# Decoding weights in pairs, and moving additions, splits and products from GpSimd to VectorE, in a kernel of decay attention and two feed-forwards

## The chip, the cores and the metric

The kernel runs on one core of a Trainium2 chip. The metric is the device time of one execution in microseconds (us); for the kernel before, three runs gave 1018.64 to 1020.18 us, median 1019.32.

## The reference

Three parts follow one another, all in float32 (inputs r, k, v are 4 x 8 x 768 x 48; the tokens are 3072, the model width 384):

```
state = w * state + k_t v_t^T                       # for every batch and head, 768 steps
y_t   = r_t (state + (u * k_t) v_t^T)
x  = (h * clip(h + 3, 0, 6) / 6) @ w_out,  h = y @ w_in       # 384 -> 2048 -> 384
out = (sigmoid(x @ w_gate) * (x @ w_val)) @ w_out2            # 384 -> 1536 -> 384
```

The weights come as float64. The kernel gets them as pairs of 32-bit words and makes float32 of them itself.

## The kernel before, in words

**Products.** A float32 matrix product is made of three float32r products (high x high, high x low, low x high), so every operand is split into a high part (a rounded copy) and a low part (the rest, a subtraction). A weight tile `w` holds both parts of 128 x 384 weights.

**Decoding.** `fetch` loads one tile of 128 x 384 doubles (`raw`, 384 KB). `decode` moves tiles through three slots. First slot: ScalarE reads the high words (`a`, L74) and the low words (`e`, L75). Second slot: VectorE clamps (L81), shifts (L83), puts the sign in (L85), each an instruction for each tile in the slot, and GpSimd adds the rounding (L87). Third slot: ScalarE copies the high part into `w` (L126), VectorE subtracts for the low part (L137). There are 68 tiles: 32 for the first feed-forward (kinds "i" and "o", two per step f), 36 for the second ("g", "v", "p").

**Attention.** The 24 chunks of 128 tokens go in the order (place in the sequence, batch). For each chunk `prep` has parts: 0 scales r and k by powers of the decay (VectorE, L272) and multiplies r by k and by u (GpSimd, L273, L274); 1 sums over a head (VectorE, L280); 2 puts the sums on reversed diagonals `ae` and `ao` (ScalarE L291, GpSimd L287 for `ao` of chunks 0 to 7); 3 scales the keys (GpSimd, L293). Stage A is 8 products and two masked copies on VectorE (L304, L305). Stage U adds to the state `Zc` on VectorE (L327, L328), and ScalarE then copies the two halves into a block-diagonal matrix `Zd` (L330). Stage Y multiplies `Zd` with r (four products of 112 x 112), then adds `ae` and `ao` times v, and sends the result through `ysb` (L349) and four small DMAs (L354) into the feed-forward's input `xf`.

**Order.** The schedule is by hand (`manual_schedule`): every engine runs its instructions in the order in which the code emits them, and so does the queue of DMA issues on SyncE. Ahead of the first feed-forward step ("the head") stand the loads, chunks 0 to 3 and six calls of `slots(1)`. Then come 6 blocks of 512 tokens with 16 steps each, and 6 blocks of the second feed-forward with 12 steps each. A step i of the first feed-forward emits: the product `h` (9 matmuls), ReLU on ScalarE (L521), `t` on VectorE (L522), the split of `t` into `gh` (ScalarE, L386) and `gl` (GpSimd, L387), a stage of attention (one per step in steps 2 to 13, in the order A, U, Y), the products `o` of step i-2, and in the first block `slots(2)`, which moves two tiles. At a block's end `split_x` splits the next input (L366, L367). In the last block of the first feed-forward `slots(1)` moves the second's tiles, then `slots(2)` in the second's first block.

Below, t_0 is the VectorE instruction `t` of step 0, t_16 that of step 16, the first of the second block.

Of the kernel before, what the change touches and what calls it, by code (L numbers as in the profile page):

```python
# [19 lines left out]
P = 128  # L20
# [8 lines left out]
# High words of doubles, read as float32: the largest and the smallest within float32's range.  # L29
# [3 lines left out]
# The chunks scale by powers from -64 to 128 of the decays; other decays go step by step.  # L33
# [4 lines left out]
LAG = 2  # L38

# [10 lines left out]
def decay_attention_ffn_ffn(ctx, tc, rkT, vkr, wT, uN, uT, flip_d, ident_d, mask_d, w_in, w_out, w_gate, w_val, w_out2, out):  # L50
# [5 lines left out]
    w_in, w_out, w_gate, w_val, w_out2 = (w.bitcast(U32) for w in (w_in, w_out, w_gate, w_val, w_out2))  # L56

    def cols_of(w, f):
        return w[:, 2 * f * P:2 * (f + 1) * P].rearrange("(k p) f -> p k f", p=P)

    def rows_of(w, f):
        return w[f * P:(f + 1) * P, :].rearrange("p (k f) -> p k f", k=1)

    def source(kind, f):
        """128 x 384 doubles as pairs of words, low word first."""
        w = {"i": w_in, "o": w_out, "g": w_gate, "v": w_val, "p": w_out2}[kind]
        return rows_of(w, f) if kind in "op" else cols_of(w, f)

    def load_words(raw, kind, f):
        src = source(kind, f)  # L70
        nc.sync.dma_start(out=raw.rearrange("p (k f) w -> p k (f w)", k=src.shape[1]), in_=src)
# [31 lines left out]
    # Tokens by block: the same 128 places of each of the four sequences.  # L103
# [6 lines left out]
    win, wout, wga, wva, wo2 = {}, {}, {}, {}, {}  # L110
    raws = {}

    def fetch(key, pool):
        raws[key] = pool.tile([P, DM, 2], U32, tag="w", name="raw")
        load_words(raws[key], *key)

    # Decoding runs over three slots: the words are read, joined to a float32, and split.
    pipe = [[], []]

    def decode(keys):  # L120
        """Starts `keys` (if any) and moves the tiles before them on by a slot."""
        old, mid = pipe
        ws = []
        for k, p, a in old:
            w = p.tile([P, 2, DM], F32R, tag="w", name="w")
            nc.scalar.activation(w[:, 0, :], a.bitcast(F32), AF.Copy)  # L126
            ws.append(w)
        new = []
        for key, pool in keys:
            raw = raws.pop(key)  # L130
            na = dec_p.tile([P, DM], U32, tag="a", name="a")
            nr = dec_e.tile([P, DM], U32, tag="e", name="e")
            read_words(na, nr, raw)
            new.append((key, pool, na, nr, raw))
        join_words(*(m[2:] for m in mid))
        for (k, p, a), w in zip(old, ws):
            nc.vector.tensor_tensor(out=w[:, 1, :], in0=a.bitcast(F32), in1=w[:, 0, :].bitcast(F32), op=ALU.subtract)  # L137
            {"i": win, "o": wout, "g": wga, "v": wva, "p": wo2}[k[0]][k[1]] = w
        pipe[:] = [m[:3] for m in mid], new

    todo_w = []
    for f in range(F1 + LAG):
        todo_w += [("i", f)] * (f < F1) + [("o", f - LAG)] * (f >= LAG)
    N1 = len(todo_w)
    for f in range(F2 + LAG):
        todo_w += [("g", f), ("v", f)] * (f < F2) + [("p", f - LAG)] * (f >= LAG)
    count = {"fetched": 0, "begun": 0}

    def fetch_next(n, pool):
        for _ in range(n):  # L150
            if count["fetched"] < len(todo_w):
                fetch(todo_w[count["fetched"]], pool)
                count["fetched"] += 1

    def slots(n, early=None, n_early=0):
        keys = []
        for _ in range(n):
            b = count["begun"]
            if b < count["fetched"]:
                keys.append((todo_w[b], early if b < N1 + n_early and b >= N1 else wpool))  # L160
                count["begun"] += 1
        if keys or any(pipe):
            decode(keys)

# [8 lines left out]
    def load_chunk(c):  # L173
        """Chunks go by their place in the sequence, and through the batch for each."""
# [3 lines left out]
        pool, tags = (wpool, ("w", "w")) if c < B else (a3, ("kr", "v"))  # L178
        kr = pool.tile([C, 2, H, D], F32, tag=tags[0], name="kr")
        v = pool.tile([C, H, D], F32, tag=tags[1], name="v")  # L180
        rows = slice(at * C, (at + 1) * C)
        nc.sync.dma_start(out=kr.rearrange("p x h d -> p (x h d)"), in_=vkr[rows, DM:3 * DM])
        nc.sync.dma_start(out=v.rearrange("p h d -> p (h d)"), in_=vkr[rows, 0:DM])
        loads[c] = t, kr, v
# [13 lines left out]
    Zc = [acon.tile([ROWS, NP, D], F32, name=f"Zc{i}") for i in range(B)]  # L198
    Zd = [acon.tile([ROWS, NP, ROWS], F32, name=f"Zd{i}") for i in range(B)]
# [9 lines left out]
    def powers():  # L209
        """W holds w^(i - 64)."""  # L210
# [18 lines left out]
        for z in Zd:  # L229
            nc.gpsimd.memset(z, 0.0)  # L230

    def powers_ahead():
        """Returns w^(i + 64)."""
# [14 lines left out]
    def find_outside():  # L248
        """Whether any decay is one that the chunks can't take."""
# [13 lines left out]
    def prep(c, part):  # L263
        """In three parts, each of which needs what the one before it left on other engines."""
        if c >= n_chunks:
            return
        if part == 0:
            t, kr, v = loads.pop(c)
            k, r = kr[:, 0], kr[:, 1]
# [3 lines left out]
            nc.gpsimd.tensor_tensor(out=r, in0=r, in1=k, op=ALU.mult)  # L273
            nc.gpsimd.tensor_tensor(out=r, in0=r, in1=uB, op=ALU.mult)  # L274
# [6 lines left out]
        elif part == 2:  # L281
            for i, nm in enumerate(("ae", "ao")):
                pool, tag = (wpool, "w") if c < B else (a2, nm)
                q[nm] = pool.tile([C, NP, C], F32, tag=tag, name=nm)
                cs = q["c"].rearrange("p (n x) -> p n x", x=2)[:, :, i:i + 1]
                if c < 2 * B and i:
                    nc.gpsimd.tensor_tensor(out=q[nm], in0=flip.rearrange("p (o t) -> p o t", o=1).to_broadcast([P, NP, C]),  # L287
                                            in1=cs.to_broadcast([C, NP, C]), op=ALU.mult)
                else:
                    for p in range(NP):  # L290
                        nc.scalar.activation(q[nm][:, p, :], flip, AF.Copy, scale=cs[:, p, :])  # L291
        elif c // B < NCH - 1:
            nc.gpsimd.tensor_tensor(out=q["k"], in0=q["k"], in1=WN, op=ALU.mult)  # L293
# [14 lines left out]
    def wide(t, h):  # L308
        """64 columns from head h on: the last 16 are the next head's, for rows that nothing uses."""
        return t.rearrange("p h d -> p (h d)")[:, h * D:h * D + 64]  # L310

    def stage_U(c, pool=ps_y, tag="y"):
# [9 lines left out]
        def after():  # L322
# [6 lines left out]
            for x in (0, 64):  # L329
                nc.scalar.activation(Zd[b][x:x + D, :, x:x + D], z[x:x + D], AF.Copy)  # L330
# [4 lines left out]
    def stage_Y(c, blk, off):  # L335
# [37 lines left out]
    def proj_into(ps, w, x, n, a=0):  # L373
        """A bank's later columns follow its first, and so leave out the start."""
# [8 lines left out]
    def split_g(g, n):  # L383
# [3 lines left out]
        nc.gpsimd.tensor_tensor(out=gl[:, :n], in0=g[:, :n], in1=gh[:, :n].bitcast(F32), op=ALU.subtract)  # L387
# [18 lines left out]
    def run_stage(c, s):  # L406
        """Emits the tensor engine's part; returns what follows it on the others."""
# [23 lines left out]
    def fetch1(n):  # L431
        fetch_next(max(0, min(n, N1) - count["fetched"]), wpool)
# [4 lines left out]
    fetch1(9)  # L437
    powers()
    on_a, on_y = {}, {}
    for c in range(B):  # L440
# [7 lines left out]
        if c > 0:  # L448
            on_a[c - 1]()
            on_y[c - 1] = stage_Y(c - 1, *chunk_of[c - 1])  # L450
            slots(1)
# [5 lines left out]
    slots(1)  # L457
# [8 lines left out]
    slots(1)  # L466
# [5 lines left out]
    slots(1)  # L472
    prep(3, 3)
    load_chunk(B)
    fetch1(13)
# [30 lines left out]
    EARLY = 9  # L506
# [10 lines left out]
    for i, (j, f) in enumerate(steps1):  # L517
# [5 lines left out]
        gs[i] = split_g(t, n)  # L523
# [11 lines left out]
        if i < F1 + 1:  # L535
            slots(2)
            fetch1(2 * i + 18)
# [241 lines left out]
```

## Time and profile before

| | |
|---|---|
| runs shown, median (range) | 1019.32 us (1018.64 to 1020.18) |
| profiled execution: its span, all that the profile gives of its time | 1017.9 us |
| TensorE busy | 963.0 us (95%) |
| VectorE, ScalarE, GpSimd busy | 440.1, 391.2, 412.9 us (43%, 38%, 41%) |
| moved by DMA | 72.10 MB |

The median lies 1.4 us above the span. A busy share is a mean over stages with different limits; what bounds a stage is read from that stage's own rows. TensorE's clock is given as the share of full speed that was granted.

### The profile page before, as it was taken

Reading aid. Unit: us, or ns where it says so; the run is one execution under the profiler, and the core shown is the slowest. Engines: PE = TensorE matmul, PEld = TensorE weight load, DVE = VectorE, ACT = ScalarE, POOL = GpSimd, SP = SyncE. Lnnn points to the kernel's source line nnn. Section 1 sums busy time; section 2 is a strip of 40 time slices with the busy share of each in tenths; the row PEclk is TensorE's granted clock in tenths of the full one; section 3 lists DMA queues with packets and bytes.
Section 4 is the critical chain, followed back from the end, with each engine's and each line's share of the span. In section 5 each row is a group of like instructions: output and inputs, shape, how many; then the busy total and the mean of one; then the engine's idle time right before and its main releaser. Section 6 shows DMA issues by size and latency. Waiting matters only on the chain.

```text
span 1017.9 us, 13297 instructions
## 1 busy us (share of the span) xinstructions
PE 963.0 (95%) x5160; PEld 807.0 (79%) x5160; DVE 440.1 (43%) x693; ACT 391.2 (38%) x792; POOL 412.9 (41%) x320
## 2 busy tenths in 40 slices
PE   4768889999999999999999998999999999999997
PEld 3546667888888888888888887889889888888886
DVE  5798886324333423421598899212112112113111
ACT  2556665344434533442475754211211212212211
POOL 4588886433543343332376665222222221221221
PEclk9688889999999999999999999999999999999999
DMA  9774213222212222200532331100100100100001
GB/s 245 229 234 143 81 50 95 61 74 81 76 50 74 81 75 65 89 8 16 185 107 65 134 133 60 62 1 1 62 1 17 46 1 29 34 1 32 1 1 34
DMA packets 49975, 72.10 MB, mean 71 GB/s; under 512 B 4848, under 2 KB 35952, under 8 KB 49904
## 3 DMA queue, kind: packets, MB, share of 16 engines
q1 hardware_dynamic: 49904, 71.18, 22.8%
q8 instruction: 42, 0.69, 0.3%
q14 instruction: 29, 0.24, 0.1%
HBM read 57.00 MB, written 9.44 MB: 65 GB/s over the span
## 4 chain that ended last, share of the span: by engine, by line
PE 78%; DVE 10%; POOL 5%; DMA 3%; ACT 2%; issue 1%; SPq 0%; DVEq 0%; POOLq 0%; ACTq 0%
PE o L107 30%; PE h L107 29%; PE pv L107 13%; PE y L107 3%; DVE w L137 3%; DVE a L85 3%; POOL gl L387 2%; PE A L107 2%; DVE a L81 2%; POOL a L87 1%; DMA raw<-in_w_in 1%; DVE a L83 1%; POOL kr L273 1%; DMA kr<-in_vkr 1%; PE U L107 1%
## 5 line engine op out<-in xcount | busy, mean ns | idle before, releaser
L387 POOL TENSOR_TENSOR gl<-t,gh 128x512 fp32r<-128x512 f32 x168 | 248.6, 1480 | 549.2 <-ACT gh L386 538.1
L107 PE MATMUL h<-xhi,w 128*128 128x512 f32 (+1 forms) x1020 | 348.3, 397 | 22.0 <-DVE w L137 18.3
L107 PEld LDWEIGHTS h<-xhi,w 128*128 128x128 f32 x1020 | 195.3, 193 | 64.5 <-DVE w L137 20.0
L386 ACT ACTIVATE gh<-t 128x512 fp32r<-128x512 f32 x168 | 106.3, 632 | 254.5 <-DVE t L594 159.0
L107 PE MATMUL h<-xlo,w 128*128 128x512 f32 (+1 forms) x510 | 202.2, 396 | 0.7 <-DVE xlo L367 0.5
L107 PE MATMUL o<-gh,w 128*128 128x512 f32 x576 | 199.1, 403 | 0.8 <-DVE w L137 0.5
L594 DVE TENSOR_TENSOR t<-t,pv 128x512 f32<-128x512 f32 x72 | 49.4, 686 | 307.3 <-PE pv L107 306.7
L522 DVE SCALAR_TENSOR_TENSOR t<-t,h 128x512 f32<-128x512 f32 x96 | 65.8, 686 | 223.3 <-ACT t L521 223.3
L107 PE MATMUL o<-w,gh 128*128 128x384 f32 x576 | 147.7, 336 | 1.5 <-DVE w L137 1.5
L107 PE MATMUL pv<-xhi,w 128*128 128x512 f32 x432 | 144.8, 389 | 1.6 <-DVE w L137 1.6
L107 PEld LDWEIGHTS o<-gh,w 128*128 128x128 f32 x576 | 108.8, 189 | 29.4 <-issue 2.6
L521 ACT ACTIVATE t<-h,three 128x512 f32<-128x512 f32 x96 | 65.5, 682 | 137.0 <-PE h L107 136.8
L107 PE MATMUL o<-gl,w 128*128 128x512 f32 x288 | 113.7, 395 | 1.4 <-POOL gl L387 1.4
L107 PEld LDWEIGHTS h<-xlo,w 128*128 128x128 f32 x510 | 98.2, 192 | 20.0 <-DVE xlo L367 1.7
L107 PEld LDWEIGHTS o<-w,gh 128*128 128x128 f32 x576 | 105.6, 188 | 6.9 <-DVE w L137 2.1
L107 PE MATMUL o<-w,gl 128*128 128x384 f32 x288 | 97.0, 337 | 0.0
L87 POOL TENSOR_TENSOR a<-a,e 128x384 uint32<-128x384 uint32 x68 | 83.4, 1239 | 32.9 <-DVE a L85 24.8
L107 PEld LDWEIGHTS pv<-xhi,w 128*128 128x128 f32 x432 | 81.0, 188 | 19.1 <-DVE w L137 2.0
L593 ACT ACTIVATE t<-h 128x512 f32<-128x512 f32 x72 | 43.0, 597 | 136.0 <-PE h L107 136.0
L107 PE MATMUL pv<-xlo,w 128*128 128x512 f32 x216 | 84.0, 389 | 0.0
L137 DVE TENSOR_TENSOR w<-a,w 128x384 fp32r<-128x384 f32 x68 | 72.1, 1085 | 6.4 <-ACT w L126 6.4
L107 PEld LDWEIGHTS o<-gl,w 128*128 128x128 f32 x288 | 54.4, 189 | 12.2 <-POOL gl L387 2.4
(69 smaller groups left out, 892.9 us busy)
## 6 DMA issues: line engine op xcount, KB each, us to landing
rk<-in_rkT SPq DMA_DIRECT2D x24, 448.0 KB, 3.8
raw<-in_w_out SPq DMA_DIRECT2D x28, 384.0 KB, 5.6
kr<-in_vkr SPq DMA_DIRECT2D x24, 384.0 KB, 3.6
raw<-in_w_in SPq DMA_DIRECT2D x16, 384.0 KB, 8.6
v<-in_vkr SPq DMA_DIRECT2D x24, 192.0 KB, 3.9
x<-ob SPq DMA_DIRECT2D x18, 256.0 KB, 2.1
raw<-in_w_gate SPq DMA_DIRECT2D x12, 384.0 KB, 3.7
raw<-in_w_val SPq DMA_DIRECT2D x12, 384.0 KB, 3.8
```

What stands on the lines that cost most here:

```text
L81: nc.vector.tensor_scalar(out=af, in0=af, scalar1=TOP, scalar2=BOTTOM, op0=ALU.min, op1=ALU.max)
L83: nc.vector.tensor_scalar(out=a, in0=a, scalar1=3, scalar2=0x3FFFFFF8, op0=ALU.logical_shift_left, op1=ALU.bitwise_and)
L85: nc.vector.scalar_tensor_tensor(out=a, in0=raw[:, :, 1], scalar=0xC0000000, in1=a, op0=ALU.bitwise_and, op1=ALU.bitwise_or)
L87: nc.gpsimd.tensor_tensor(out=a, in0=a, in1=r, op=ALU.add)
L107: nc.tensor.matmul(o, l, r, start=start, stop=stop, skip_group_check=True)
L137: nc.vector.tensor_tensor(out=w[:, 1, :], in0=a.bitcast(F32), in1=w[:, 0, :].bitcast(F32), op=ALU.subtract)
L386: nc.scalar.activation(gh[:, :n], g[:, :n], AF.Copy)
L387: nc.gpsimd.tensor_tensor(out=gl[:, :n], in0=g[:, :n], in1=gh[:, :n].bitcast(F32), op=ALU.subtract)
L521: nc.scalar.activation(t[:, :n], ps[:, :n], AF.Relu, bias=three)
L522: nc.vector.scalar_tensor_tensor(out=t[:, :n], in0=t[:, :n], scalar=6.0, in1=ps[:, :n], op0=ALU.min, op1=ALU.mult)
L593: nc.scalar.activation(t[:, :n], pg[:, :n], AF.Sigmoid)
L594: nc.vector.tensor_tensor(out=t[:, :n], in0=t[:, :n], in1=pv[:, :n], op=ALU.mult)
```

## The change

Seven things, by their places in the code:

- The weights lie in memory in the order of use, two tiles side by side (the host writes them so). One DMA of 768 KB loads a pair, with one run of 6 KB for each partition; before, a tile of `w_in`, `w_gate` or `w_val` came in runs of 1 KB. `slot()` moves one pair (128 x 768) through the three slots.
- The rounding is added by VectorE instead of GpSimd.
- `gl` is made by VectorE in steps 0 to 17, by GpSimd after that.
- The products of `prep` parts 0 and 3 are made by VectorE for chunks 0 to 7; `ao` is always made by ScalarE.
- A chunk's k, r and v are loaded by one DMA.
- `Zd` and its copies are gone: stage Y multiplies the two 48-row halves of `Zc` with r in two 64-row, 64-column parts of the array, so it has eight products where there were four.
- The head's six slots start six pairs (12 tiles; before, six tiles), the loop of step 0 starts none, steps 1 to 10 start one each. In the last block of the first feed-forward a slot comes at every second step.

```diff
-        for a, r, raw in tiles:
-            nc.gpsimd.tensor_tensor(out=a, in0=a, in1=r, op=ALU.add)
+        for a, r, raw in tiles:
+            nc.vector.tensor_tensor(out=a, in0=a, in1=r, op=ALU.add)
...
+    def decode(i, pool):
         old, mid = pipe
+        new = None
+        if old:
+            k, p, a = old
+            w = p.tile([P, 2, 2 * DM], F32R, tag="w", name="w")
             nc.scalar.activation(w[:, 0, :], a.bitcast(F32), AF.Copy)
+        if i is not None:
+            raw = raws.pop(i)
+            na = dec_p.tile([P, 2 * DM], U32, tag="a", name="a")
+            nr = dec_e.tile([P, 2 * DM], U32, tag="e", name="e")
             read_words(na, nr, raw)
+            new = i, pool, na, nr, raw
+        if mid:
+            join_words(mid[2:])
+        if old:
             nc.vector.tensor_tensor(out=w[:, 1, :], in0=a.bitcast(F32), in1=w[:, 0, :].bitcast(F32), op=ALU.subtract)
...
+                raws[i] = pool.tile([P, 2 * DM, 2], U32, tag="w", name="raw")
+                nc.sync.dma_start(out=raws[i].rearrange("p f w -> p (f w)"), in_=wst[i])
...
-            nc.gpsimd.tensor_tensor(out=r, in0=r, in1=k, op=ALU.mult)
-            nc.gpsimd.tensor_tensor(out=r, in0=r, in1=uB, op=ALU.mult)
+            side = nc.vector if c < 2 * B else nc.gpsimd
+            side.tensor_tensor(out=r, in0=r, in1=k, op=ALU.mult)
+            side.tensor_tensor(out=r, in0=r, in1=uB, op=ALU.mult)
...
-            nc.gpsimd.tensor_tensor(out=q["k"], in0=q["k"], in1=WN, op=ALU.mult)
+            side = nc.vector if c < 2 * B else nc.gpsimd
+            side.tensor_tensor(out=q["k"], in0=q["k"], in1=WN, op=ALU.mult)
...
-            for x in (0, 64):
-                nc.scalar.activation(Zd[b][x:x + D, :, x:x + D], z[x:x + D], AF.Copy)
...
-                mm(ps[0:ROWS, p, :], Zd[b][:, p, :], q["R"][:, p, :], p == 0, False)
+                mm(ps[0:64, p, :], Zs[b][0:D, p * D:p * D + 64], q["R"][0:D, p, :], p == 0, False)
+                mm(ps[64:64 + D, p, :], Zc[b][64:64 + D, p, :], q["R"][64:64 + D, p, :], p == 0, False)
...
-        nc.gpsimd.tensor_tensor(out=gl[:, :n], in0=g[:, :n], in1=gh[:, :n].bitcast(F32), op=ALU.subtract)
+        side.tensor_tensor(out=gl[:, :n], in0=g[:, :n], in1=gh[:, :n].bitcast(F32), op=ALU.subtract)
...
-    fetch1(9)
+    fetch1(4)
...
-            fetch1(8 + c)
+            fetch1(3 + c)
...
-        gs[i] = split_g(t, n)
+        gs[i] = split_g(t, n, nc.vector if i < F1 + 2 else nc.gpsimd)
...
-            slots(2)
-            fetch1(2 * i + 18)
+            slot()
+            fetch1(i + 9)
...
-        if i >= last:
-            slots(1, w2pool, EARLY)
+        if i >= last and f % 2 == 1:
+            slot(w2pool, EARLY)
             fetch_next(1, w2pool)
...
-        slots(2, w2pool, EARLY)
-        fetch_next(2, w2pool)
+        slot(w2pool, EARLY)
+        fetch_next(1, w2pool)
```

## Rows read from the trace of the kernel before

**Rows 1.** Busy times by stretch: span, then each engine, granted clock, DMA share, GB/s
```profile
48.92:171.78 122.86, 98.44 (x554) 75.93 (x554) 106.60 (x166) 72.25 (x162) 101.68 (x67) 0.87 0.42 126
180.00:486.00 306.00, 306.00 (x1859) 247.50 (x1857) 101.44 (x162) 131.34 (x277) 116.41 (x96) 1.00 0.21 61
559.87:638.37 78.50, 75.45 (x361) 65.56 (x361) 73.64 (x110) 44.12 (x92) 44.71 (x34) 1.00 0.31 106
```

**Rows 2.** Chain that ended last, two pieces in the first block: start, length, what
```profile
104.81 5.20 POOL gl L387
...
128.29 5.20 POOL gl L387
```

**Rows 3.** VectorE in order of time, first block, two tiles in the slot
```profile
129.29 0.62 DVE L81 TENSOR_SCALAR a<-a 128x384 f32<-128x384 f32 x2
129.83 0.62 DVE L83 TENSOR_SCALAR a<-a 128x384 uint32<-128x384 uint32 x2
130.37 1.02 DVE L85 SCALAR_TENSOR_TENSOR a<-raw,a 128x384 uint32<-128x384 uint32 x2
131.30 1.02 DVE L137 TENSOR_TENSOR w<-a,w 128x384 fp32r<-128x384 f32 x2
```

**Rows 4.** The same view, second feed-forward's first block, GpSimd at work
```profile
600.25 2.12 DVE L85 SCALAR_TENSOR_TENSOR a<-raw,a 128x384 uint32<-128x384 uint32 x2
```

**Rows 5.** The same view, head, one tile in the slot
```profile
40.43 0.35 DVE L81 TENSOR_SCALAR a<-a 128x384 f32<-128x384 f32 x1
40.81 0.36 DVE L83 TENSOR_SCALAR a<-a 128x384 uint32<-128x384 uint32 x1
41.21 0.56 DVE L85 SCALAR_TENSOR_TENSOR a<-raw,a 128x384 uint32<-128x384 uint32 x1
41.69 0.55 DVE L137 TENSOR_TENSOR w<-a,w 128x384 fp32r<-128x384 f32 x1
```

**Rows 6.** The chain, one step of the first block: from t to gl
```profile
80.10 0.70 DVE t L522
80.82 0.64 ACT gh L386
...
81.53 4.94 POOL gl L387
```

**Rows 7.** VectorE in order of time, first block: attention and split
```profile
144.23 0.35 DVE L327 TENSOR_TENSOR Zc<-Zc,W 112x192 f32<-112x192 f32 x1
...
152.08 1.22 DVE L272 TENSOR_TENSOR rk<-rk,W 112x1024 f32<-112x1024 f32 x1
...
156.76 0.75 DVE L304 COPY_PREDICATED ae<-mask,A 128x512 f32<-128x512 uint32 x1
...
167.30 0.69 DVE L367 TENSOR_TENSOR xlo<-xf,xhi 128x512 fp32r<-128x512 f32 x1
```

**Rows 8.** ScalarE in order of time, head: four of the scaled diagonals
```profile
30.37 1.28 ACT L291 ACTIVATE ae<-flip,cd 128x128 f32<-128x128 f32 x4 [3.04 <-DVE cd L280]
```

**Rows 9.** ScalarE in order of time, head: reads of the first two weight tiles
```profile
23.81 0.54 ACT L74 ACTIVATE a<-raw 128x384 f32<-128x384 f32 x1 [5.88 <-DMA raw<-in_w_in]
...
25.87 0.54 ACT L74 ACTIVATE a<-raw 128x384 f32<-128x384 f32 x1
```

**Rows 10.** The chain, head: issue and landing of the attention's result
```profile
36.69 0.57 SPq L354
...
37.30 2.44 DMA xf<-ysb
```

**Rows 11.** The chain, end of the first block and after: nine products each
```profile
168.92 2.04 PE h L107 x9
...
183.19 2.27 PE o L107 x9
```

**Rows 12.** TensorE in order of time, third block: parts of stages Y and A
```profile
335.75 1.04 PE L107 MATMUL y<-rk,Zd 112*112 112x128 f32 x8
...
342.08 1.16 PE L107 MATMUL A<-rk 64*128 64x128 f32 x16
```

More of the change, by code (lines that the diff above doesn't have):

```diff
@@ L38, with weight_order @@
 LAG = 2
+def weight_order():
+    todo = []
+    for f in range(F1 + LAG):
+        todo += [("i", f)] * (f < F1) + [("o", f - LAG)] * (f >= LAG)
+    for f in range(F2 + LAG):
+        todo += [("g", f), ("v", f)] * (f < F2) + [("p", f - LAG)] * (f >= LAG)
+    return [tuple(todo[i:i + 2]) for i in range(0, len(todo), 2)]
+PAIRS = weight_order()
+NP1 = F1
 def starts(blocks):
@@ L49, in decay_attention_ffn_ffn @@
 @with_exitstack
-def decay_attention_ffn_ffn(ctx, tc, rkT, vkr, wT, uN, uT, flip_d, ident_d, mask_d, w_in, w_out, w_gate, w_val, w_out2, out):
+def decay_attention_ffn_ffn(ctx, tc, rkT, vkr, wT, uN, uT, flip_d, ident_d, mask_d, wst, out):
     nc = tc.nc
@@ L54, in decay_attention_ffn_ffn @@
     main = ExitStack()
[L56 to L67, printed above, removed]
+    wst = wst.bitcast(U32)
+    place = {key: (i, x) for i, pair in enumerate(PAIRS) for x, key in enumerate(pair)}
     def load_words(raw, kind, f):
-        src = source(kind, f)
-        nc.sync.dma_start(out=raw.rearrange("p (k f) w -> p k (f w)", k=src.shape[1]), in_=src)
+        i, x = place[kind, f]
+        nc.sync.dma_start(out=raw.rearrange("p f w -> p (f w)"), in_=wst[i, :, 2 * x * DM:2 * (x + 1) * DM])
     def read_words(a, r, raw):
@@ L110, in decay_attention_ffn_ffn @@
     win, wout, wga, wva, wo2 = {}, {}, {}, {}, {}
+    parts = {"i": win, "o": wout, "g": wga, "v": wva, "p": wo2}
     raws = {}
[L113 to L120, printed above, removed]
+    pipe = [None, None]
+    def decode(i, pool):
         old, mid = pipe
-        ws = []
-        for k, p, a in old:
-            w = p.tile([P, 2, DM], F32R, tag="w", name="w")
+        new = None
+        if old:
+            k, p, a = old
+            w = p.tile([P, 2, 2 * DM], F32R, tag="w", name="w")
             nc.scalar.activation(w[:, 0, :], a.bitcast(F32), AF.Copy)
[L127 to L132, printed above, removed]
+        if i is not None:
+            raw = raws.pop(i)
+            na = dec_p.tile([P, 2 * DM], U32, tag="a", name="a")
+            nr = dec_e.tile([P, 2 * DM], U32, tag="e", name="e")
             read_words(na, nr, raw)
-            new.append((key, pool, na, nr, raw))
-        join_words(*(m[2:] for m in mid))
-        for (k, p, a), w in zip(old, ws):
+            new = i, pool, na, nr, raw
+        if mid:
+            join_words(mid[2:])
+        if old:
             nc.vector.tensor_tensor(out=w[:, 1, :], in0=a.bitcast(F32), in1=w[:, 0, :].bitcast(F32), op=ALU.subtract)
[L138 to L146, printed above, removed]
+            for x, (kind, f) in enumerate(PAIRS[k]):
+                parts[kind][f] = w[:, :, x * DM:(x + 1) * DM]
+        pipe[:] = mid and mid[:3], new
     count = {"fetched": 0, "begun": 0}
@@ L150, in fetch_next, with slot @@
         for _ in range(n):
-            if count["fetched"] < len(todo_w):
-                fetch(todo_w[count["fetched"]], pool)
+            i = count["fetched"]
+            if i < len(PAIRS):
+                raws[i] = pool.tile([P, 2 * DM, 2], U32, tag="w", name="raw")
+                nc.sync.dma_start(out=raws[i].rearrange("p f w -> p (f w)"), in_=wst[i])
                 count["fetched"] += 1
[L155 to L163, printed above, removed]
+    def slot(early=None, n_early=0):
+        i = count["begun"]
+        if i < count["fetched"]:
+            decode(i, early if NP1 <= i < NP1 + n_early else wpool)
+            count["begun"] += 1
+        elif any(pipe):
+            decode(None, None)
     att = ExitStack()
@@ L177, in load_chunk @@
         nc.sync.dma_start(out=t, in_=rkT[:, at])
[L178 to L184, printed above, removed]
+        pool, tag = (wpool, "w") if c < B else (a3, "vkr")
+        n = pool.tile([C, 3, H, D], F32, tag=tag, name="vkr")
+        nc.sync.dma_start(out=n.rearrange("p x h d -> p (x h d)"), in_=vkr[at * C:(at + 1) * C, :])
+        loads[c] = t, n
     w_given = keep.tile([ROWS, NP, 1], F32, name="w_given")
@@ L197, in decay_attention_ffn_ffn @@
     pw = acon.tile([ROWS, NP, 1], F32, name="pw")
-    Zc = [acon.tile([ROWS, NP, D], F32, name=f"Zc{i}") for i in range(B)]
-    Zd = [acon.tile([ROWS, NP, ROWS], F32, name=f"Zd{i}") for i in range(B)]
+    Zs = [acon.tile([ROWS, NP * D + 16], F32, name=f"Z{i}") for i in range(B)]
+    Zc = [z[:, :NP * D].rearrange("p (n d) -> p n d", n=NP) for z in Zs]
     nc.sync.dma_start(out=w_given.rearrange("p n o -> p (n o)"), in_=wT)
@@ L228, in powers @@
         v.tensor_tensor(out=W[:, :, 0:M], in0=F, in1=bc(W128)(M), op=ALU.mult)
-        for z in Zd:
-            nc.gpsimd.memset(z, 0.0)
+        for z in Zs:
+            nc.gpsimd.memset(z[:, NP * D:], 0.0)
     def powers_ahead():
@@ L281, in prep @@
         elif part == 2:
+            pool, tag = (wpool, "w") if c < B else (a2, "aeo")
+            ab = pool.tile([C, 2, NP, C], F32, tag=tag, name="aeo")
             for i, nm in enumerate(("ae", "ao")):
-                pool, tag = (wpool, "w") if c < B else (a2, nm)
-                q[nm] = pool.tile([C, NP, C], F32, tag=tag, name=nm)
+                q[nm] = ab[:, i]
                 cs = q["c"].rearrange("p (n x) -> p n x", x=2)[:, :, i:i + 1]
[L286 to L291, printed above, removed]
+                for p in range(NP):
+                    nc.scalar.activation(q[nm][:, p, :], flip, AF.Copy, scale=cs[:, p, :])
         elif c // B < NCH - 1:
-            nc.gpsimd.tensor_tensor(out=q["k"], in0=q["k"], in1=WN, op=ALU.mult)
+            side = nc.vector if c < 2 * B else nc.gpsimd
+            side.tensor_tensor(out=q["k"], in0=q["k"], in1=WN, op=ALU.mult)
     def stage_A(c):
@@ L381, in proj_into, with split_g @@
         return ps
-    def split_g(g, n):
+    def split_g(g, n, side):
         gh = g_p.tile([P, 512], F32R, tag="gh", name="gh")
@@ L450, in decay_attention_ffn_ffn @@
             on_y[c - 1] = stage_Y(c - 1, *chunk_of[c - 1])
-            slots(1)
+            slot()
         if c > 1:
             on_y[c - 2]()
-            fetch1(8 + c)
+            fetch1(3 + c)
     on_a[B - 1]()
     on_y[B - 1] = stage_Y(B - 1, *chunk_of[B - 1])
-    slots(1)
+    slot()
     HALF = 2 * C
@@ L465, in decay_attention_ffn_ffn @@
     prep(1, 3)
-    slots(1)
+    slot()
     after_u()
@@ L471, in decay_attention_ffn_ffn @@
     split_x(0, xf.pop(0), BLOCKS1[0], HALF)
-    slots(1)
+    slot()
     prep(3, 3)
     load_chunk(B)
-    fetch1(13)
+    fetch1(6)
     load_chunk(B + 1)
@@ L762 @@
         "mask": np.ascontiguousarray(np.triu(np.ones((P, P), np.uint32), 1)[::-1]),
-        "w_in": words(w_in),
-        "w_out": words(inputs["moe_w_out"]),
-        "w_gate": words(inputs["moe2_w_gate"]),
-        "w_val": words(inputs["moe2_w_val"]),
-        "w_out2": words(inputs["moe2_w_out"]),
+        "weights": words(np.stack([np.concatenate([tile_of(*key) for key in pair], axis=1) for pair in PAIRS])),
     }
```

27 lines of the change are left out of this document (17 added, 10 removed).

## The prediction

> **What bounds the kernel now.** I read the busy times by stretch first. From 180 to 486 us TensorE is busy in all of 306.00 us, and the other engines are far below that [rows 1]: there only TensorE's own work counts. Two stretches are different. In the first block, from t_0 at 48.92 to t_16 at 171.78 (122.86 us), TensorE works 98.44 us while VectorE works 106.60 and GpSimd 101.68 [rows 1]. In the second feed-forward's first block TensorE loses 78.50 - 75.45 = 3.05 us [rows 1]. All that can be won by faster decoding lies in the head and in these two.
>
> Then the chain and VectorE's timeline in the first block. The chain passes through GpSimd's `gl` at 104.81 and again three steps later at 128.29, 5.20 us each time [rows 2]; so three steps take 23.5 us. GpSimd and VectorE hold each other up: two signs (L85) take 1.02 us while GpSimd leaves VectorE alone [rows 3] and 2.12 us beside GpSimd's work [rows 4], and a `gl` that takes 5.20 us in the chain is a subtraction of 512 columns, which VectorE does in 0.69 [rows 7]. The two engines together are one resource, and it is full.
>
> **What VectorE will need.** With GpSimd idle in this stretch I price everything at VectorE's undisturbed durations. An instruction that doesn't need the one before it starts about 0.08 us before that one's end (129.29 + 0.62 and the start at 129.83 [rows 3]); one that does starts after it. A pair is one tile of 768 columns, so clamp, shift, sign and rounding now follow from one another, with no second tile between them. From the single tiles: 0.35, 0.36 and 0.56 us, starts 0.38, 0.40, 0.48 apart [rows 5]. 384 columns more cost 0.2 us in clamp and shift (0.27 a tile when two alternate [rows 3], less 0.07 of start) and 0.4 in the two-input kinds (0.47 a tile). So clamp 0.58, shift 0.59, sign 0.99, rounding 0.87: the join takes 3.03, and with the low part (0.87) a pair takes 3.90 us. The rounding on VectorE isn't in the trace; its bounds are the sign and the low part (0.47 to 0.57 for 384 columns), which are the same shape, so I take these.
>
> - `t` and `gl`: `gl` stands right behind `t` in VectorE's queue but needs `gh`. From the start of `t` to the start of `gl` passed 1.43 us (80.10 to 81.53, with ScalarE's 0.64 between [rows 6]); VectorE now stands still for it, and all that is emitted after `gl` (masked copies, join, low part) waits too. With `gl` itself at 0.61 (0.69 less 0.08 [rows 7]): 2.04 a step.
> - Attention: two masked copies 1.3, sum and key scaling 0.47 each (384 columns, as a low part) in a step with A: 2.2. State 0.7 (two of 0.35) in a step with U. Scaling 1.14, two products of 384 columns 0.58 + 0.47 in a step with Y: 2.2 [rows 5, 7].
>
> **The loop, step by step.** Step 0 (no new pair; state, chunk 4's products): 2.04 + 0.3 + 3.90 + 2.2 = 8.4. Step 1: 2.04 + sum 0.47, then the low part must wait for the copy of the high part, which stands on ScalarE behind eight diagonals (two times 1.28 [rows 8]) and takes some 0.9 itself (0.64 for 512 columns [rows 6]); with low part, chunk 5's products and key scaling: 9.5. Step 2 (A, no low part) 7.3. Then U 6.65, Y 8.15 and A 8.15 in turn: steps 3 to 9 are 3 x 6.65 + 4 x 8.15 = 52.6. Step 10 (Y, products of chunk 8 left on GpSimd) 7.1, step 11 (A without key scaling) 7.7. In the U steps ScalarE (eight diagonals, two reads, one copy, ReLU) needs some 0.2 more than VectorE: 0.6. Sum t_0 to t_12: 93.2 us. So a step still costs what it did, (6.65 + 8.15 + 8.15) against 23.5 for three; the gain is that the last pair is done in step 12 and that TensorE has meanwhile run ahead.
>
> TensorE then has step 13's products behind it. Up to t_16 it has three `h` (2.04 each), four `o` (2.27 each [rows 11]), A (1.16 [rows 12]) and a U (16 pieces too, of 48 columns instead of 128, I take 0.6): 17.0, and with the first `t` (0.7) and the last ReLU (about 0.6, as `gh`) 18.3 us. GpSimd's products in steps 10 and 11 disturb VectorE again: 1 us. So t_0 to t_16 takes 93.2 + 18.3 + 1.0 = 112.5 instead of 122.86: **-10.4 us** (bounds: 0 for the disturbance, TensorE not ahead, which costs one `h` and one `o` more: -11.4 to -6.1).
>
> **The head.** It gets longer, for it now decodes twice as many tiles. The first tile's read starts at 23.81, when it has landed, the second's at 25.87 [rows 9]; the first pair is as many bytes as both, so it lands between these; I take 25.0, and VectorE starts on it one read later (0.54 + 0.3), at 25.8. From there its queue is full: five joins 15.2, four low parts 3.5, chunk 3's scaling, products and sum 2.8, four masked copies 2.6, the split of 512 columns 4.0 (six casts and six subtractions of 256, at the rates above), four key scalings 1.9, state 0.6: 30.6 us. t_0 comes at 56.4, against 48.92, where the stretch of [rows 1] begins: **+7.5 us** (bounds from the landing: +6.3 to +8.3). What hides nothing here is said plainly: the products taken from GpSimd cost VectorE 3.1 us of these, which GpSimd did beside it.
>
> **The second feed-forward's first block.** VectorE needs 0.6 + 3.90 a step, and beside a `gl` left on GpSimd some 1.1 more (2.12 less 1.02 [rows 3, 4]): 5.6, under TensorE's step of 27 products of about the size of three `h`, 6.1 [rows 11], and three more. So the 3.05 us of idle TensorE go, but not all: the slots every second step leave one pair fewer done ahead of the block, and pair 16 of it is finished in step 10 for use in step 11; VectorE needs 0.7 + 3.9 from TensorE's end of step 10, TensorE has an `o` and an `h` to do meanwhile, some 4.2, and a `gl` may add 1.1. I take 1.2 lost: **-1.9 us** (bounds -3.05 to 0).
>
> **At nothing.** `Zd`'s copies: ScalarE is busy 72.25 of 122.86 us there [rows 1]; without that cover they would be two copies of 192 columns a chunk. Eight small products instead of four: in stage A, two halves of the array work side by side, 16 pieces in 1.16 us, and Zd's 8 took 1.04 [rows 12]. So 16 pieces should take about as long (between 1.04 and 2 x 1.04; I take the first, as the row of A is the nearest). Fewer and longer DMAs: a pair's load is issued three steps, over 20 us, before its read in the loop, and ahead of t_0 only the first one is waited for. GpSimd is left with `gl` from step 18 on, as before.
>
> **Sum.** 7.5 - 10.4 - 1.9 = -4.8. Against the profiled span of 1017.9 that is 1013.1; the median of the runs lies 1.4 above it: **1014.5 us**.
>
> **Rivals.**
> - *Chained instructions cost nothing extra.* Then a pair takes 0.47 + 0.47 + 3 x 0.87 = 3.55, 0.35 less, some 15 times on the path: 5.3 us more gain, 1009.2. Against it stand the single tiles' starts, 0.38 to 0.48 apart where two alternating tiles give 0.27 and 0.47 [rows 3, 5]; for it, that 768 columns may hide a fixed wait. The Trainium skill, page "VectorE: DVE Perf Modes", section "The DRAIN you can't avoid", holds that the pipe is emptied after each instruction whether or not a semaphore stands between, so that chaining costs no more than independence; by that it would be this rival's time. This trace disagrees by about 0.1 us for each clamp and shift. Chance 0.08.
> - *The head eats it all.* The head has no slack at one point: the split of the first 256 columns comes up at about 41.9, and its data leave ScalarE only after the third pair's reads, at about 37, with four DMA issues of about 0.6 and a landing of 2.44 behind [rows 10]: 42. Each us later is a us on t_0. With 3 to 5 us the gain is gone: 1018 to 1020. For it: in-order reads on ScalarE stand ahead of `ysb`. Chance 0.13.
> - *ScalarE becomes the bound.* ReLU stands behind three 768-column instructions and, in U steps, eight diagonals. If it is 0.7 late in each of 12 steps, +8.4: 1023. Against it: 72 of 123 us busy before [rows 1], less the `Zd` copies. Chance 0.07.
> - *The small products don't overlap (slower).* Place: stage Y in the stretch where TensorE is busy all the time, 16 chunks. If the 64 x 64 parts work one after the other, 16 pieces take 2.08 for 1.04 [rows 12], +1.04 x 16 = 16.6 us: 1031. It decides from 0.3 us a chunk on. Against it: stage A. Chance 0.06.
> - *The change doesn't do what it says* (GpSimd's disturbance remains, since its later work moves into the block): about 1019. Chance 0.02.
>
> **How the numbers follow.** The forecast has 0.64. Its own range is 1010 to 1018. For the whole I take 1008 to 1022: it holds the first rival and the second and leaves out the fourth and part of the third. About 0.2% (2 us) is what a measurement of this kernel can tell from no change. Faster: 0.9 of the forecast's 0.64, the first rival's 0.08 and a little of the second, 0.68; same 0.13; slower 0.19 (the third and fourth, half of what is left of the second, and the forecast's tail).
>
> **What would show it.** In the profile after: t_0 at about 56 and t_16 at about 168; VectorE's L81, L83, L85 and L87 for 768 columns near 0.55, 0.56, 0.96, 0.95; `gl` on VectorE with an idle 0.7 before it, released by `gh`; steps of 6.7 to 8.2 us up to step 12, then TensorE without gaps; stage Y's 16 pieces in about 1.1; a second feed-forward's first block of 75 to 77 us. I am wrong if steps 2 to 11 take 5 to 6 us (then VectorE isn't the bound I take it for), if t_0 is past 60, or if the stretch from the second block to the sixth changes its length.

## The result, and the profile after

| | before | after |
|---|---|---|
| runs side by side, median (range) | 1019.75 us (1018.64 to 1020.31) | 1024.06 us (1023.07 to 1026.54) |
| span of the profiled execution | 1017.9 us | 1024.8 us (the run of 1026.54) |
| VectorE, GpSimd busy | 440.1, 412.9 us | 430.6, 247.8 us |

The ratio is 1.0051, 95% interval [1.0036, 1.0065]: slower by 4.3 us, against a forecast of 4.8 us faster. The profiled execution of after was its slowest run, so its 6.9 us more of span are 2.6 more than the medians differ by.

Busy times by stretch of the kernel after: t_0 to t_16 and its two parts (cut at t_12), the second block, and the second feed-forward's first block. Columns as in [rows 1], and the first three and the last of these answer to the first and last row there:

```profile
53.70:175.60 121.90, 96.29 (x583) 75.53 (x583) 96.98 (x140) 62.20 (x118) 10.29 (x8) 0.86 0.34 108
53.70:147.12 93.42, 71.89 (x431) 56.30 (x431) 79.92 (x116) 49.83 (x90) 4.27 (x3) 0.85 0.38 125
147.12:175.60 28.48, 24.40 (x153) 19.22 (x152) 17.07 (x25) 12.37 (x28) 6.02 (x5) 0.88 0.20 56
258.49:341.37 82.88, 82.88 (x548) 65.93 (x544) 29.53 (x47) 33.70 (x70) 33.74 (x28) 1.00 0.24 70
565.31:642.97 77.66, 75.41 (x361) 65.67 (x361) 70.01 (x82) 43.64 (x62) 17.54 (x12) 1.00 0.34 112
```

The same cut in the kernel before:

```profile
48.92:143.63 94.71, 71.96 (x412) 55.54 (x413) 85.66 (x128) 54.92 (x121) 83.34 (x56) 0.86 0.47 142
143.63:171.78 28.15, 26.48 (x144) 20.40 (x142) 20.94 (x39) 17.34 (x41) 18.34 (x11) 0.88 0.23 71
```

So in the profiled executions: head +4.78 (t_0 at 53.70 for 48.92), t_0 to t_16 -0.96, the blocks between t_16 and t_80 +1.62 (327.29 for 325.67), the second feed-forward's first block -0.84: +4.60. The rest of the 6.9 stands behind the last output (below).

VectorE in order of time, kernel after: its start on the first pair in the head, a pair in step 0, two rows of step 8, and the tail of the first block:

```profile
22.86 0.56 DVE L86 TENSOR_SCALAR a<-a 128x768 f32<-128x768 f32 x1 [2.56 <-ACT a L79]
...
55.96 0.55 DVE L86 TENSOR_SCALAR a<-a 128x768 f32<-128x768 f32 x1
56.54 0.56 DVE L88 TENSOR_SCALAR a<-a 128x768 uint32<-128x768 uint32 x1
57.14 0.96 DVE L90 SCALAR_TENSOR_TENSOR a<-raw,a 128x768 uint32<-128x768 uint32 x1
58.13 0.96 DVE L92 CUSTOM_DVE_ANT_0 a<-a,e 128x1536 uint16<-128x1536 uint16 x1
59.01 0.95 DVE L139 TENSOR_TENSOR w<-a,w 128x768 fp32r<-128x768 f32 x1
...
122.52 1.74 DVE L92 CUSTOM_DVE_ANT_0 a<-a,e 128x1536 uint16<-128x1536 uint16 x1
124.19 1.74 DVE L139 TENSOR_TENSOR w<-a,w 128x768 fp32r<-128x768 f32 x1
...
147.12 0.68 DVE L514 SCALAR_TENSOR_TENSOR t<-t,h 128x512 f32<-128x512 f32 x1
148.50 1.30 DVE L379 TENSOR_TENSOR gl<-t,gh 128x512 fp32r<-128x512 f32 x1 [0.70 <-ACT gh L378]
149.72 1.15 DVE L320 TENSOR_TENSOR Z<-Z,W 112x192 f32<-112x192 f32 x1
150.97 0.35 DVE L321 TENSOR_TENSOR Z<-Z,U 112x192 f32<-112x192 f32 x1
...
154.43 1.22 DVE L266 TENSOR_TENSOR rk<-rk,W 112x1024 f32<-112x1024 f32 x1
161.08 0.69 DVE L514 SCALAR_TENSOR_TENSOR t<-t,h 128x512 f32<-128x512 f32 x1 [5.44 <-ACT t L513]
```

The join takes 3.05 us from 55.96 to 59.01; 3.03 had been costed. In the tail, t_12 at 147.12 has `gl` behind it, `gl` waits for ScalarE, and only then comes the update of Z that empties U's bank, at 150.97. TensorE at the same time, in order of time:

```profile
151.38 1.97 PE L112 MATMUL y<-rk,Z 48*64 48x128 f32 x16 [4.08 <-DVE Z L321]
153.28 1.97 PE L112 MATMUL y<-aeo,vkr 128*64 128x128 f32 x16
```

Y (of another batch than this Z, so it needs the bank and not the value) stands still until Z is through; then VectorE stands still 5.44 us ahead of t_14. The two engines work in turns. TensorE's waits from t_0 to t_16 (for what; us in total, times, longest):

```profile
PE y L112 <- DVE Z L321: 14.4, 3, 5.6
PE y L112 <- DVE Z L318: 6.5, 1, 6.5
PE h L112 <- DVE t L514: 3.2, 2, 2.1
PE A L112 <- DVE rk L266: 2.9, 1, 2.9
```

No weight tile is in that list: the decoded weights are no longer late for TensorE. VectorE's attention work is, which stands in VectorE's queue between the joins and behind `gl`. After the wait the granted clock is at half, the 1.2 GHz level, and then full again (windows; the last three figures are the clock, the DMA share and GB/s):

```profile
146.91:151.38 4.47, 0.39 (x2) 0.00 (x1) 3.62 (x5) 3.55 (x10) 3.39 (x3) 0.83 0.00 0
151.38:156.90 5.52, 5.52 (x36) 4.53 (x37) 3.38 (x4) 1.96 (x4) 0.00 (x0) 0.52 0.00 1
156.90:161.36 4.46, 4.46 (x32) 3.48 (x30) 0.28 (x1) 0.69 (x1) 0.00 (x0) 1.00 0.56 135
```

### The profile page after: what moved, and what is told of

It reads as the page before. It is cut to its first block, busy times and chain, and to the rows that moved or that the text cites. A ratio compares the mean times of both kernels' runs of the same rounds, so it can differ in the third digit from the quotient of the medians.

```text
span 1024.8 us, 13160 instructions
## 1 busy us (share of the span) xinstructions
PE 962.6 (94%) x5320; PEld 805.8 (79%) x5320; DVE 430.6 (42%) x633; ACT 377.0 (37%) x682; POOL 247.8 (24%) x202
## 4 chain that ended last, share of the span: by engine, by line
PE 84%; DVE 11%; ACT 2%; issue 1%; DMA 1%; SPq 0%; DVEq 0%; ACTq 0%
PE o L112 32%; PE h L112 31%; PE pv L112 14%; PE y L112 4%; PE A L112 2%; DVE a L90 2%; DVE w L139 2%; DMA raw<-in_weights 1%; DVE a L88 1%; ACT gh L378 1%; DVE gl L379 1%; DVE t L514 1%; DVE a L92 1%; PE U L112 1%; DVE a L86 1%
## 5 line engine op out<-in xcount | busy, mean ns | idle before, releaser
L112 PE MATMUL h<-xhi,w 128*128 128x512 f32 (+1 forms) x1020 | 343.5, 392 | 7.9 <-DVE xhi L358 4.7
L379 POOL TENSOR_TENSOR gl<-t,gh 128x512 fp32r<-128x512 f32 x150 | 201.4, 1343 | 601.4 <-ACT gh L378 599.0
L283 ACT ACTIVATE aeo<-flip,cd 128x128 f32<-128x128 f32 x192 | 58.5, 387 | 4.9 <-DVE cd L275 4.9
L268 POOL TENSOR_TENSOR vkr<-vkr 128x384 f32<-128x384 f32 x16 | 16.4, 1028 | 161.5 <-DMA vkr<-in_vkr 161.5
```

Source lines behind the costliest of these rows:

```text
L112: nc.tensor.matmul(o, l, r, start=start, stop=stop, skip_group_check=True)
L268: side.tensor_tensor(out=r, in0=r, in1=k, op=ALU.mult)
L379: side.tensor_tensor(out=gl[:, :n], in0=g[:, :n], in1=gh[:, :n].bitcast(F32), op=ALU.subtract)
```

## Experiments: who holds the tail

Four corners: U's bank (where its products land; U and Y share one) moved or not, `gl` late or not.

**U in another bank** (label a_ubank), on the kernel after:

```
-        f = stage_A(c) if s == 0 else stage_U(c) if s == 2 else stage_Y(...)
+        f = stage_A(c) if s == 0 else stage_U(c, ps_a, "A") if s == 2 else stage_Y(...)
```

> The kernel after, with the state products U of the loop's stages written to a bank of the A pool and no longer to the one bank that U and Y share. Theory 1 (the shared bank): Y of one step can't begin until VectorE has emptied U of the step before, and VectorE does that only behind its split of g; TensorE, which works in order, idled 4.1 to 6.5 us four times ahead of Y in the first block. With U in another bank those idles fall below 1.5 us each, t_12 to t_16 (28.48 us after) comes to 18 to 21, and the whole to 1014 to 1018 us. Theory 2 (the weights, that is VectorE's decode, set the tail and the wait for Z only stands where TensorE would have waited for a weight tile anyway): the idles move to the products of h and o, t_12 to t_16 stays at 26 to 29 and the whole within 2 us of 1024.

Measured 1022.32 us, ratio to before 1.0028 [1.0018, 1.0039]. The whole is in theory 2's range, the tail between the two. Parts and waits of its first block:

```profile
56.18:149.26 93.08, 70.98 (x424) 55.64 (x425) 79.61 (x116) 49.43 (x90) 4.01 (x3) 0.85 0.36 124
149.26:172.86 23.60, 23.60 (x161) 18.49 (x159) 16.47 (x26) 12.27 (x28) 5.92 (x5) 1.00 0.22 67
```
```profile
PE U L112 <- DVE aeo L297: 17.0, 4, 5.0
PE A L112 <- DVE rk L266: 4.4, 1, 4.4
PE h L112 <- DVE t L514: 1.0, 1, 1.0
```

The tail loses 4.9 us, and TensorE is busy in all of it. But the idles of the steps before don't go: they move ahead of U (the last is 5.0 us, ahead of 144.44), which now needs the bank that VectorE's masked copy of A empties. Whichever bank it is, TensorE's next stage there stands behind VectorE's work of this step.

**The same edit on the kernel before** (b_ubank):

> The kernel before with the same one edit (U of the loop's stages in a bank of the A pool). Theory 1: the bank is shared there too, so its own 28.15 us from t_12 to t_16 also shrink, by 3 to 8 us, and the whole to 1012 to 1017 us; then the bank is a cost that both kernels carry and that hid the change's gain. Theory 2: no change, 1018 to 1021 us, since in this kernel GpSimd (83 of 95 us busy up to t_12) delivers g's low part and the decoded tiles too late for TensorE to gain by it.

1018.40 us, 0.9997 [0.9988, 1.0006]: no change, as theory 2 had it; t_12 to t_16 stays at 27.76. In that kernel TensorE waits 16.2 us for decoded weights (L137) in the first block.

**`gl` behind the join** (a_gl_late), where it goes to VectorE; the bank left as it was:

```
 in split_g:  -  side.tensor_tensor(out=gl..., op=ALU.subtract)
              +  lows.append(lambda: side.tensor_tensor(out=gl..., op=ALU.subtract))
 in the loop: slot()
              +  while lows: lows.pop(0)()
```

> The kernel after with g's low part of the first block emitted behind the join of the next tiles, U left in the bank that it shares with Y: the fourth corner beside the kernel after, the bank alone and both. Theory 1 (TensorE and VectorE work in turns in the tail because VectorE comes to t_12 a step behind and TensorE's next stage stands behind its work, whichever bank that is): VectorE comes out of the decode earlier, t_0 to t_12 is 86 to 88 us as with both, and t_12 to t_16 falls to 23 to 26 even with the shared bank; whole 1015 to 1018. Theory 2 (the shared bank by itself holds the tail): t_12 to t_16 stays at 27 to 29 and the whole is 1017 to 1020.

1013.81 us, 0.9950 [0.9936, 0.9964]: faster than both kernels by one move in a queue.

```profile
54.36:141.59 87.23, 73.43 (x429) 57.35 (x430) 80.11 (x117) 49.60 (x90) 4.26 (x3) 0.83 0.39 131
141.59:165.43 23.84, 22.44 (x156) 17.67 (x154) 16.13 (x26) 12.26 (x28) 5.25 (x5) 1.00 0.25 76
```

Theory 1 on both parts; the whole came out 1.2 us below its range. VectorE's `gl` now starts with no wait; the end of a pair, `gl` and the next `t` (order of time; here L520 is `t`):

```profile
110.70 0.95 DVE L139 TENSOR_TENSOR w<-a,w 128x768 fp32r<-128x768 f32 x1
111.57 0.68 DVE L379 TENSOR_TENSOR gl<-t,gh 128x512 fp32r<-128x512 f32 x1
112.17 0.68 DVE L520 SCALAR_TENSOR_TENSOR t<-t,h 128x512 f32<-128x512 f32 x1
```

**Both** (a_ubank_gl_late):

> The kernel after with U in a bank of the A pool, and g's low part in the first block emitted on VectorE behind the join of the next tiles and no longer right behind t, so that VectorE doesn't stand 0.70 us a step for ScalarE's high part. Theory 1 (VectorE's own queue sets the steps): t_0 to t_12 falls by the 8.4 us of that idle to 84 to 86, and with the bank's 8 to 10 us the whole comes to 1005 to 1010. Theory 2 (g's low part now comes 5 to 6 us later to the second products, which TensorE takes in order): what VectorE saves TensorE loses, and the whole stays within 2 us of the run with the bank alone.

1013.87 us, 0.9957 [0.9944, 0.9971]: neither theory's time. The steps came 0.4 us above theory 1's range and the whole 3.9.

```profile
56.16:142.53 86.37, 73.17 (x453) 57.05 (x455) 79.78 (x117) 49.43 (x90) 5.25 (x5) 0.88 0.40 134
142.53:162.79 20.26, 20.26 (x134) 16.14 (x130) 14.75 (x26) 12.17 (x28) 4.40 (x4) 1.00 0.31 102
```

The tail is 20.26 us, TensorE busy in all of it. The four corners of t_12 to t_16 are 28.48, 23.60, 23.84 and 20.26: either edit takes some 4.8 us, both 8.2. Each is one profiled execution; where neither edit touches it, the same part took 28.48, 28.36 (a_zd) and 27.02 (a_nofb), so it varies by up to 1.5 us from one execution to another. The medians with both and with `gl` alone are equal, though the profiled span with both is 2.6 us shorter (1011.9 for 1014.5; that of a_gl_late was its slowest run). So in the medians the bank alone is worth 0.23% (1.0051 to 1.0028, with intervals that overlap), and beside the late `gl` nothing. The head of the execution with both is the later one, t_0 at 56.16 for 54.36. In a_ubank, whose t_0 is as late (56.18), VectorE waits 1.60, 1.29 and 0.75 us for the chunks' loads and 3.11 for the first pair; in the kernel after 0.77 and 1.23, then 2.56. So landings move the head by about 2 us from one profiled execution to another; the edit to the bank is none to the head, and a_best, which has it too, has t_0 at 53.83. How much of the bank's gain they hide in the medians stays open.

## Experiments: the other parts

**`gl` on GpSimd in the first block** (a_gl_pool), that part undone (`side` is GpSimd for every step):

> The kernel after with g's low part in the first block back on GpSimd, that part alone undone. Theory 1 (VectorE sets t_0 to t_12: 79.9 of 93.4 us busy, 8.3 of them in the split of g and 8.4 idle ahead of it for ScalarE's high part): VectorE loses 16.7 us there and gets back some for operations that run beside GpSimd, so t_0 to t_12 falls to 80 to 87 us and the whole to 1011 to 1019. Theory 2 (operations beside GpSimd cost VectorE what it saves, the decode's 2x rows of 0.95 to 1.74 us being the sign): t_0 to t_12 stays at 91 to 97 and the whole at 1022 to 1027.

1015.87 us, 0.9972 [0.9963, 0.9981]; t_0 to t_12 86.69, t_12 to t_16 24.69. Theory 1. Without the rounding and the products GpSimd's `gl` takes 1.27 to 2.01 us (62.92 to 83.67), no longer the 5.20 of [rows 2]; VectorE pays for it at places (L88 1.66 for 0.56), less than it saves. So moving `gl` undid what the rest of the change had won.

**Products of chunks 0 to 7 on GpSimd** (a_prod_pool):

> The kernel after with the element products of chunks 0 to 7 (r by k, by u, and k by the decay table) back on GpSimd, that part alone undone. Theory 1 (VectorE sets the first block, and these are 13 of its operations, 7.2 us of 93.4): VectorE loses 7 us from t_0 to t_12 and the whole falls to 1018 to 1021, unless the head, where chunks 0 to 3 are on the path to the first products, gets 1 to 3 us longer by GpSimd's slower operations. Theory 2 (an operation beside GpSimd costs VectorE 0.6 us more, as its rows of 1.74 for 0.95 show at two places): what VectorE saves it loses in the decode, t_0 to t_12 stays above 91 and the whole at 1023 to 1028.

1023.26 us, 1.0044 [1.0030, 1.0058]; t_0 to t_12 89.97, t_0 at 54.72. On the steps neither theory: they lose 3.5 us, half of what was moved. The whole is in theory 2's range, within 0.8 of the kernel after. It is a part of little weight.

**Block-diagonal state kept** (a_zd), in two buffers that ScalarE fills in stage A's second part:

```
+    Zd = [acon.tile([ROWS, NP, ROWS], F32, ...) for i in range(2)]
-    mm(ps[0:64, p, :], Zs[b][0:D, ...], q["R"][0:D, p, :], ...); mm(ps[64:64 + D, p, :], Zc[b][64:64 + D, p, :], ...)
+    mm(ps[0:ROWS, p, :], Zd[c % 2][:, p, :], q["R"][:, p, :], p == 0, False)
```

> The kernel after with the block-diagonal copies of the state kept (two buffers, filled by ScalarE two copies a chunk when the chunk's A is done) and 4 full-width products in place of 8 narrow ones per chunk. Theory 1 (the narrow products cost TensorE about 0.1 us a chunk wherever it sets the pace): the five later blocks of the first feed-forward fall from 82.88 to about 82.5 us each, and the whole by 1.2 to 2 us, to 1022 to 1023. Theory 2 (the 0.4 us per block come from something else, such as the operations that moved off GpSimd): blocks stay at 82.9, whole within 0.6 us of 1024, or above by ScalarE's copies.

1023.38 us, 1.0043 [1.0029, 1.0056]. Its third block, and its row of Y beside that of the kernel after:

```profile
257.16:339.64 82.48, 82.48 (x515) 66.59 (x514) 29.54 (x48) 36.06 (x78) 33.74 (x28) 1.00 0.23 71
...
338.66 1.04 PE L112 MATMUL y<-rk,Zd 112*112 112x128 f32 x8
```
```profile
340.48 1.08 PE L112 MATMUL y<-rk,Z 48*64 48x128 f32 x16
```

From t_16 to t_80 it takes 325.64 us, as before (325.67), for 327.29 after: theory 1 in the profile, 0.1 us a chunk. The medians differ by 0.7 only, and their ranges overlap.

**The section behind the last output** (b_nofb, a_nofb: the conditional path for decays out of range is left out of either kernel, with its test):

> The kernel before without the conditional section that follows the last output (the path for decays out of range; it isn't taken with these inputs, and here its code and its test are left out). Theory 1 (what lies between the last output's copy and the end of the span belongs to that section's code): the 6.0 us from the last copy of an output to the end of the span shrink to the landing of the last store, some 2 to 4 us, and the whole falls by 2 to 4, to 1015 to 1017. Theory 2 (it is the end of the program whatever its code): 1018.5 to 1019.5, the end still 6.0.

> The kernel after without the same section. Theory 1: its end (8.3 us in the profile, 7.9 to 8.5 in the kernels made from it) shrinks to the same 2 to 4 us as in the kernel before without it, so the whole falls by 4 to 6, to 1018 to 1020, and the two kernels without the section stand 2 to 3 us apart where the full ones stand 4.9 apart. Theory 2: the end stays at 8 us, the whole at 1023.5 to 1024.5.

1014.65 us, 0.9958 [0.9945, 0.9972], and 1020.29 us, 1.0016 [1.0007, 1.0025], ten of a_nofb's eleven runs lying at 1019.0 to 1022.2. The last copy of an output, after, in a span of 1024.8 us, and in a_nofb, span 1017.5:

```profile
1016.01 0.49 ACT L575 ACTIVATE ob<-o 128x384 f32<-128x384 f32 x1 [0.61 <-PE o L112]
```
```profile
1014.22 0.49 ACT L575 ACTIVATE ob<-o 128x384 f32<-128x384 f32 x1 [0.61 <-PE o L112]
```

From its end to the end of the span are 8.3 us after (6.0 before, 6.5 in b_ubank, 7.9 to 8.5 in every other kernel made from after that keeps the section), but 2.8 in a_nofb and 2.9 in b_nofb. So the end does belong to the section, though it isn't taken, and its part is 2.3 us longer after. But the second half of theory 1 fell: the two kernels without it stand 5.6 us apart, not closer. Their profiled spans differ by 5.3: head +7.3 (b_nofb's t_0 is at 46.40), first block -2.6, blocks +1.6, second feed-forward -0.9. The medians don't show the 2.3 us: by the ratios the section is worth 0.42% of the kernel before (4.3 us) and 0.35% of the kernel after (3.6).

**All three edits, and fewer slots ahead of the loop** (a_best: bank, `gl` late, Zd; a_best_slot5 and a_best_slot4 leave out one and two of the last head calls of `slot()` too):

> The kernel after with three edits: U in a bank of the A pool, g's low part of the first block behind the join, and the block-diagonal state kept. If the three add up: 1013.9 less about 1.5, so 1011.5 to 1013. If the block-diagonal copies on ScalarE delay the first block (its decode passes stand behind them): 1013.5 to 1016.

> The three edits together (U's bank, g's low part behind the join, block-diagonal state), and one decoding slot fewer ahead of the first block: five, so that the loop has one more, at a step where TensorE waits less. Theory 1 (VectorE's work is one sum, wherever it stands): the first t comes 4 us earlier and the sixteenth at the same time, whole within 1 us of 1011. Theory 2 (VectorE has idle time in the tail, from t_12 to t_16, that a later decode fills): t_16 comes 2 to 4 us earlier, whole 1007 to 1009. Against both: a weight tile late to its product would add 1 to 3 us.

> The same with two slots fewer, four ahead of the first block. Theory 1: as with five, whole within 1 us of 1011. Theory 2: t_0 8 us earlier, and t_16 4 to 6 us earlier than with six, whole 1005 to 1008. If the weight tiles come late instead (PE's products of h waiting for the split), the gain is given back and the whole is 1010 to 1015.

1011.03 us (0.9924 [0.9911, 0.9938]), 1011.43 (0.9918 [0.9905, 0.9932]) and **1006.37 us (0.9872 [0.9857, 0.9887])**, 12.6 below the runs of before beside it. The three together come out 0.5 us below the range in which they were to add up. With five slots theory 1 held for the whole, but not in its parts; with four theory 2's size came, but its place isn't shown. In the profiled executions t_0 is at 53.83, 51.20 and 49.27, t_16 at 160.36, 162.34 and 159.43. That of six slots was its fastest run (1009.42) and that of four its slowest (1008.63), so these two runs differ by 0.8 us only, and where the 4.7 us between the medians come from stays open. The last one's waits of TensorE from t_0 to t_16 have no weight tile:

```profile
PE U L112 <- DVE aeo L298: 14.6, 5, 5.4
PE A L112 <- DVE rk L267: 2.0, 1, 2.0
```

## Why the prediction was wrong

- **The failed step** is the sentence "TensorE then has step 13's products behind it", with "the gain is that the last pair is done in step 12 and that TensorE has meanwhile run ahead". It gave 18.3 us for t_12 to t_16 (19.3 with the disturbance); 28.48 were measured. Even the bound for "TensorE not ahead", 23.6, was short. The chain through the tail of the kernel after (start, length, what) is below. It has 4.26 us from t_12 until Y starts (0.7 had been put for t_12 itself; the rest is `gl`'s wait, `gl` and the update of Z), Y 3.86 and `o` 2.97 that were to be done already (2.03 and 2.27 at full clock, so 2.5 us of it is the clock), then 16.56 for the products that I counted at 17.0 (158.22 to 174.78, with U), and 0.82 to t_16. A stage of attention in every step ties TensorE to VectorE, by the banks of U and A; an engine that is tied has no lead when the other one's load ends. In the profiled executions the four corners show that both the tie (the bank) and VectorE's lateness (the wait for `gh`) count in the tail; with both eased it is 20.26. In the medians it is the lateness that counts: `gl` moved back takes 10 us off, the bank beside it nothing.

```profile
151.38 3.86 PE y L112 x30
155.24 2.97 PE o L112 x9
158.22 2.05 PE h L112 x9
160.27 1.09 PE A L112 x16
161.36 2.27 PE o L112 x9
163.63 2.04 PE h L112 x9
165.67 0.60 PE U L112 x14
166.26 6.34 PE o L112 x27
172.61 2.17 PE h L112 x9
```

- **The steps to t_12** were right in mechanism: 93.2 forecast, 93.42 measured, and the decode's rows to 0.1 us. That the sum is so close is in part luck. GpSimd's products disturbed VectorE in step 8, not in 10 and 11 (rounding and low part 1.74 each at 122.52 and 124.19, step 8 at 9.67 for 8.15), and again behind t_12 (`gl` 1.30 for 0.69, Z 1.15 for 0.35): 3.0 us in all for the 1.0 that I had put. GpSimd, which had nothing else to do, began on them when their load had landed. The 1.6 us of it in step 8 were made up by other terms that were a little high. And I took `gl`'s wait of 0.7 as given. It stood in plain sight in my sum (2.04 a step), and moving it was worth 10 us of the whole.
- **The head**: +7.5 forecast, +4.78 measured; VectorE's queue took 30.84 us for 30.6, the landing was mis-sized: VectorE started at 22.86, not 25.8 (but at 25.3 in a_ubank and with both edits). Over executions with the same head, t_0 lies at 52.92 to 56.18 after and 46.40 to 48.92 before.
- **Small products** at nothing: +0.1 us a chunk, 1.6 us, inside the bounds and far below the rival's 1.04. They do overlap.
- **The second feed-forward's first block**: -1.9 forecast, -0.84 measured. TensorE waits twice for a weight: 1.00 us at 638.69, near the 1.2 that I had put, and 1.11 at 633.11, where none was forecast. The join ahead of the second has a sign of 1.94 for 0.96 beside GpSimd's `gl` (629.26), as the joins before it have; that the sign makes this wait is argued from the times, not tried.
- **The end** behind the last output wasn't in the sum: +2.3 in the profile, not seen in the medians.
- **The chaining rival** fell: in the loop clamp, shift and sign start 0.58, 0.60 and 0.99 apart (55.96, 56.54, 57.14, 58.13). The Trainium skill, page "VectorE: DVE Perf Modes", section "The DRAIN you can't avoid", says of a chain of eight copies that a semaphore after each costs nothing extra. But it also says that a next instruction that isn't held starts earlier, which the prediction left out. This trace agrees with the second: an instruction that needs the one before it costs about 0.1 us over the 0.47 and 0.87 worked out for the rival, one that doesn't starts about 0.08 us before that one's end.
- The **other rivals**: up to t_12 VectorE waited 0.4 us in all for the ReLU, so ScalarE was no bound at the place that this rival named; the split of the first 256 columns started at 39.28 without a wait, so the attention's result didn't hold the head. GpSimd's disturbance did remain in part, by the 3.0 us above. The slower side came by a mechanism that none of them had.

In the profiled execution the misses add up: -2.7 head, +0.2 steps, +9.2 tail, +1.6 products, +1.1 second feed-forward, +2.3 end, 11.7 of the 12.0 between 1014.5 and 1026.54.

## What to carry to other kernels

Where an engine's own rate is to set the time after another engine's load ends, walk that hand-over instruction by instruction: as long as each of its steps needs a bank that the late engine empties, it has no lead to spend. An instruction that must wait for a third engine goes at the end of an in-order queue's step, not behind its producer: here 0.7 us a step, and with it one per cent of the whole. When work moves between engines, undo each part alone; here one part (`gl`) took away what the others gave. Not undone alone here were the pairs with their longer DMAs, the rounding, the chunk's single load and `ao` on ScalarE, so what each of these is worth isn't shown.

## What was not expected of the hardware

- A conditional section that isn't taken costs 3.1 us (before) and 5.5 us (after) between the last output and the end of the span, by the profiles with and without it; by the medians it is 4.3 and 3.6.
- A 192-column product on VectorE takes 1.15 us for 0.35 where GpSimd works (149.72; GpSimd's scaling of a chunk's keys runs from 149.20 to 150.65).
- After an idle of 4.08 us TensorE's clock was granted at 0.52 for the next 5.5 us, which made Y 3.86 for 2.03.
- The rounding add of 768 uint32 columns appears as a custom VectorE instruction on 1536 uint16 columns, at 0.96 us, the same as the other two-input kinds.
